# Carrying D·xn in PSUM ahead of Y, smaller first w1 loads, and a last group with tokens on partitions

## The chip, the cores and the metric

The kernel runs on one core of one Trainium2 chip. The metric is the device time of one execution in microseconds (us). A core has TensorE (PE), VectorE (DVE), ScalarE (ACT), GpSimd (POOL) and SyncE (SP, which only issues transfers here); they run their own instruction streams and meet through semaphores. PE multiplies into PSUM, an accumulator memory of 8 banks (ps0 to ps7) of 512 float32 columns; the other engines read and write PSUM and SBUF. DMA queues of SP and ACT move data between HBM and SBUF, and within SBUF with a transpose.

## The reference

x is 2048 tokens by 448 (bfloat16). A first normalization gives xn. One branch is a linear state-space scan over the tokens (448 complex states) with a skip term D, the other a normalized two-layer network, and the second gates the first:

```python
xn = _layernorm(x)                       # no weights; eps 1e-5
Lam_bar = exp(dt * Lam); B_bar = ((Lam_bar - 1) / Lam)[:, None] * B
h_t = Lam_bar * h_(t-1) + B_bar @ xn_t   # over 2048 tokens, complex
s = 2 * Re(C @ h_t) + xn * Dskip
g = silu(gelu(_layernorm(xn) @ w1 + b1) @ w2 + b2)   # 448 -> 1792 -> 448
out = x + s * g
```

## The kernel before

The tokens go in four groups of 512 (`g` = 0 to 3), each of two blocks of 256; a block is held as 128 partitions by two parities. Per group there are these stages, named by the letter that `STEPS` (L180 to L186) uses for them.

- L and N: normalization (`ln`), then a DMA transpose that puts the features on partitions: `xnT` for the scan branch, `xn2T` for the network.
- m: the first product, `mm1_phase` (matmuls L661, two phases into one pair of banks), with gelu by ACT out of PSUM into `gT` (L667).
- b: `bu_phase`, B·xn by PE (L690) with `BT`, the transposed matrix that `lb` and `bt` build (three DMA transposes: BT0, BT1, BT3, BT4 in two, and BT2, BT5, BT6 in the third); evacuated to `ue` and `u_sb`.
- S: `ssm` on DVE: table products, two scans (L749), products back into `hx`, and `hz` = hx + ue (L768).
- W: the second product, `mm2` (L783, and L786 for the last 64 features), features on partitions and 512 tokens as columns; ACT's silu with b2 as a bias column (L789) gives `g_sb`.
- Y: `yt`, for each of four blocks of features: 7 matmuls with `CZ` on hx (odd tokens, L805) and 7 with `CQ` on hz (even tokens, L806; L813 and L814 for the last 64 features). The skip term is added in one of two ways: DVE adds D·xn in a multiply-add out of PSUM into `tmp` (L826, thirteen of the sixteen), or PE adds a product with a diagonal matrix `Dg` of D (L808, L816: three of the last group). Then t3 = Y·g on DVE (L828).
- O and P: groups 0 to 2 leave by `out_dma`: two DMA transposes of t3 back to tokens, adds of x (L842, L845), stores. Group 3 leaves by `out_pe`: transposes on PE (L855), adds (L861), stores by SP and ACT in two pairs, the first of features 0 to 255, the last of 192 (rows of 384 bytes).

The gathering of work is written out in advance. Every operation is a task with the keys that it reads and writes (`Plan.add`); `ORDER` lists all task numbers once, each engine runs its tasks in that order, and `SECOND` names those that run on the second of two possible engines (`either`). So PE, in order, stands behind its first late input, and a transfer stands behind all that its queue has issued before. Just ahead of the fifth last task of SP (`settle`, L107), SP waits for all transfers that are under way.

The start: SP issues x, then w1 in five pieces (four column chunks of rows 0 to 383, `w1_0` to `w1_3`, and `w1r`, the rows 384 to 447 for all columns), then D and b2 as two rows (`drows`); ACT issues the three state vectors and b1. `skip_columns` (L554, L555) turns the two rows into columns `db` with small matmuls, which PE runs after the first 34 matmuls of the first product. `tables` makes the sine and decay tables `WT` under one key, "W"; the ten-step sine chain from L491 on runs on DVE.

## Time and profile before

| what | value |
| --- | --- |
| median of 3 runs | 147.08 us (147.01 to 148.35) |
| span of the profiled execution | 145.3 us |
| its own time beside the span | not recorded; the median lies 1.78 us above the span |
| busy: PE, DVE, ACT, POOL | 138.8, 130.1, 100.5, 26.0 us |
| the chain that ended last | PE 85%, DVE 4%, DMA 3%, SP's queue 3% |
| multiply-adds L826 on DVE | 16, 10.1 us, 645 ns each |
| moved by DMA | 15.98 MB, 110 GB/s over the span |

The profile is of one execution. A row of a group gives the line, the engine, the operation, output<-inputs, shapes and count, then the busy time and the mean of one in ns, then the idle time before them with what ended it. A row of a timeline begins with start and length in us; a bracket is the wait before it and what released it. A row of a window gives the busy time of each engine, the granted clock of PE (1.00 is full), the share of time that the DMA engines were busy, and GB/s. Matmuls overlap in the pipeline, so their own durations (380 ns for 512 columns) are longer than the step from one to the next (0.2145 us).

### The profile page before, as it was taken

Reading aid. Unit: us, or ns where it says so; the run is one execution under the profiler, and the core shown is the slowest. Engines: PE = TensorE matmul, PEld = TensorE weight load, DVE = VectorE, ACT = ScalarE, POOL = GpSimd, SP = SyncE. Lnnn points to the kernel's source line nnn. Section 1 sums busy time; section 2 is a strip of 40 time slices with the busy share of each in tenths; the row PEclk is TensorE's granted clock in tenths of the full one; section 3 lists DMA queues with packets and bytes.
Section 4 is the critical chain, followed back from the end, with each engine's and each line's share of the span. In section 5 each row is a group of like instructions: output and inputs, shape, how many; then the busy total and the mean of one; then the engine's idle time right before and its main releaser. Section 6 shows DMA issues by size and latency. Waiting matters only on the chain.

```text
span 145.3 us, 3626 instructions
## 1 busy us (share of the span) xinstructions
PE 138.8 (95%) x1457; PEld 91.9 (63%) x1461; DVE 130.1 (90%) x284; ACT 100.5 (69%) x184; POOL 26.0 (18%) x76
## 2 busy tenths in 40 slices
PE   7879999999999999999999999999999999999990
PEld 7757764464444477776768644877766668744870
DVE  2898999899999799899999999798699999999782
ACT  3588889998889466799999690594559993086200
POOL 4354315154500017000020000300000710000000
PEclk9999999999999999999999999999999999999999
DMA  4959990899999990000000074819800100201434
GB/s 104 299 173 242 351 366 19 162 226 95 210 210 215 122 241 11 5 2 5 0 0 5 18 144 89 163 23 187 192 7 0 68 0 0 82 4 23 95 116 126
DMA packets 38610, 15.98 MB, mean 110 GB/s; under 512 B 33145, under 2 KB 38146, under 8 KB 38594
## 3 DMA queue, kind: packets, MB, share of 16 engines
q1 hardware_dynamic: 38036, 15.52, 48.7%
q10 hardware_dynamic: 558, 0.24, 0.6%
q8 instruction: 11, 0.18, 0.5%
q14 instruction: 5, 0.04, 0.1%
HBM read 5.86 MB, written 1.84 MB: 53 GB/s over the span
## 4 chain that ended last, share of the span: by engine, by line
PE 85%; DVE 4%; DMA 3%; SPq 3%; issue 2%; DVEq 0%
PE psum L661 29%; PE psum L783 25%; PE psum L690 15%; PE psum L805 6%; PE psum L786 4%; PE psum L806 4%; DMA dk<-in_B_b_dram 3%; SPq L78 3%; PE psum L813 2%; DVE t L828 2%; DVE tmp L826 1%; DVE Bn L861 1%; DVE Bn L842 0%; PE psum L855 0%; PE psum L814 0%
## 5 line engine op out<-in xcount | busy, mean ns | idle before, releaser
L661 PE MATMUL psum<-xn2T,w_sb 64*128 64x512 bf16 (+1 forms) x476 | 46.7, 340 | 1.0 <-DVE w_sb L302 0.8
L667 ACT ACTIVATE gT<-psum,b1f 128x512 bf16<-128x512 f32 (+1 forms) x68 | 37.4, 615 | 5.2 <-PE psum L661 5.1
L783 PE MATMUL psum<-gT,w_sb 128*128 128x512 bf16 x164 | 36.2, 379 | 0.4 <-issue 0.3
L661 PEld LDWEIGHTS psum<-xn2T,w_sb 64*128 64x128 bf16 x476 | 25.3, 108 | 15.6 <-PE psum L661 1.4
L783 PEld LDWEIGHTS psum<-gT,w_sb 128*128 128x128 bf16 x168 | 16.2, 98 | 19.8 <-ACT gT L667 1.1
L690 PE MATMUL psum<-xnT,BT 64*128 64x256 bf16 x392 | 24.5, 270 | 0.2 <-DVE tmp L826 0.2
L690 PEld LDWEIGHTS psum<-xnT,BT 64*128 64x128 bf16 x392 | 18.9, 94 | 6.1 <-DVE tmp L826 0.4
L749 DVE TENSOR_TENSOR_SCAN s_w<-vs,dk 128x786 f32<-128x786 bf16 (+1 forms) x8 | 16.3, 2058 | 0.1
L443 ACT ACTIVATE xn_sb<-x_all,lnw 128x448 bf16<-128x448 bf16 (+2 forms) x18 | 11.2, 670 | 5.3 <-DMA xnT<-xn_sb 5.2
L301 ACT ACTIVATE vs<-s_w 64x258 bf16<-64x258 f32 (+2 forms) x12 | 8.0, 686 | 8.0 <-DVE s_w L749 7.9
L789 ACT ACTIVATE g_sb<-psum,db 128x512 bf16<-128x512 f32 (+1 forms) x16 | 9.3, 623 | 4.5 <-PE psum L783 4.4
L826 DVE SCALAR_TENSOR_TENSOR tmp<-xnT,db,psum 128x512 f32<-128x512 bf16 (+1 forms) x16 | 10.1, 645 | 0.9 <-PE psum L814 0.7
L805 PE MATMUL psum<-hx,CZ 128*128 128x256 bf16 x84 | 10.8, 276 | 0.0
L758 POOL TENSOR_TENSOR ang<-s_w,ang 128x16 f32<-128x16 f32 x3 | 1.8, 616 | 49.2 <-ACT s_w L756 49.2
L806 PE MATMUL psum<-Bn,CQ 128*128 128x256 bf16 x84 | 10.5, 273 | 0.0
L465 ACT ACT_TABLE_LOAD x8 | 10.3, 1283 | 0.3
L805 PEld LDWEIGHTS psum<-hx,CZ 128*128 128x128 bf16 x84 | 8.0, 98 | 2.5 <-issue 0.6
L301 ACT ACTIVATE ue<-psum 128x512 bf16<-128x512 f32 (+1 forms) x13 | 6.8, 549 | 3.6 <-PE psum L690 3.6
L806 PEld LDWEIGHTS psum<-Bn,CQ 128*128 128x128 bf16 x84 | 8.1, 98 | 1.4 <-issue 0.4
L301 ACT ACTIVATE u_sb<-psum 128x512 bf16<-128x512 f32 (+1 forms) x14 | 6.0, 490 | 3.5 <-PE psum L690 3.4
L828 DVE TENSOR_TENSOR t<-tmp,g_sb 128x512 bf16<-128x512 f32 (+1 forms) x13 | 7.9, 622 | 0.0
L442 DVE TENSOR_SCALAR xn_sb<-x_all,lnw 128x448 bf16<-128x448 bf16 (+2 forms) x22 | 7.2, 361 | 0.5 <-DMA xnT<-xn_sb 0.3
(155 smaller groups left out, 183.7 us busy)
## 6 DMA issues: line engine op xcount, KB each, us to landing
x_all<-in_A_x_dram SPq DMA_DIRECT2D x3, 448.0 KB, 4.6
w_sb<-in_B_w_dram SPq DMA_DIRECT2D x3, 448.0 KB, 6.4
out_dram<-Bn SPq DMA_DIRECT2D x6, 224.0 KB, 2.4
w_sb<-in_B_w_dram SPq DMA_DIRECT2D x3, 384.0 KB, 5.1
w_sb<-in_B_w_dram SPq DMA_DIRECT2D x2, 224.0 KB, 5.0
Bn<-in_A_B_im_dram SPq DMA_DIRECT2D x1, 336.0 KB, 7.5
Bn<-in_A_B_re_dram SPq DMA_DIRECT2D x1, 336.0 KB, 8.0
x_all<-in_A_x_dram SPq DMA_DIRECT2D x2, 112.0 KB, 2.0
```

Of the source, the lines that this page charges most:

```text
L301: kb.either(("act", [lambda e, o=o, i=i: e.activation(o, i, ACT.Copy) for o, i in pairs]), ("dve", [lambda e, o=o, i=i: e.tensor_copy(o, i ...
L443: ("act", [lambda e, o=o, i=i: e.activation(o, i, ACT.Identity, bias=nb, scale=rs) for o, i in parts]),
L465: kb.add("act", lambda e: e.preload_act_table_set(what), reads, writes, sem=name)
L661: return lambda e: e.matmul(dst(bk[k]), w1_sb[rows, d, fcol(2 * j + k)], rhs[rows, d], start=not second and n == 0, stop=second and n == 3)
L667: act(lambda e, k=k, fi=fi: e.activation(gT[:, gb, fi, cols], psum[:, bk[k], cols], ACT.Gelu_apprx_tanh, bias=b1f[:, fi:fi + 1]), ["b1f", ...
L690: fns.append(lambda e, rows=rows, bank=bank, m=m, o=o, n=n: e.matmul(psum[:, bank, c * NK:(c + 1) * NK].rearrange("p (b c) -> p b c", b=2) ...
L749: dve(lambda e, so=so, vi=vi, di=di: e.tensor_tensor_scan(so, vi, di, 0.0, ALU.add, ALU.mult), ["v", "vl", "vz", "dk", "dk01"] + ["v3"] * ...
L783: pe([lambda e, fi=fi: e.matmul(psum[:, bk, :], w2_sb[:, fi, 128 * j:128 * j + 128], gT[:, gb, fi, :], start=fi == 0, stop=fi == NF - 1) f ...
L805: pe([lambda e, k=k: e.matmul(par(psum[:, bk, :], 1), CZ[:, k, cols], halves(hx[:, hb, k, 1:NK + 1]), start=k == 0, stop=k == 6) for k in ...
L806: fns = [lambda e, k=k: e.matmul(par(psum[:, bk, :], 0), CQ[:, k, cols], halves(hz[:, hb, k, :]), start=not by_pe and k == 0, stop=not by_ ...
L826: dve([lambda e, o=o, p=p, x=x, d=d: e.scalar_tensor_tensor(out=v(o), in0=x, scalar=d, in1=v(p), op0=ALU.mult, op1=ALU.add) for o, p, x, d ...
L828: dve(lambda e: e.tensor_tensor(t3[:, 512 * j:512 * j + n], s, g_sb[:, hb, 512 * j:512 * j + n], ALU.mult), [ks, f"g{hb}_{j}"], [f"t3{j}"])
```

## The change

It has three parts, and a new order of everything.

1. In groups 0 to 2 the bank of Y is first written with D·xn, by ACT (ten of twelve: a copy with the D column as scale) or by DVE (two), and all matmuls then accumulate on it (`start=False`). The multiply-adds L826, the diagonal matrices `Dg` and their matmuls go; t3 is read out of PSUM.
2. `w1r` is loaded in two column pieces, 96 KB behind `w1_0` (192 KB, now first) and 128 KB behind `w1_2`. The rows of D and b2 are loaded on ACT's queue right behind b1. PE runs `skip_columns` five phases of the first product later.
3. In group 3 the second product has tokens on partitions: per quarter of 128 tokens, ACT copies a b2 row spread over all partitions into the bank, and 14 matmuls take `gT` as the stationary and w2 (448 columns) as the moving operand. Y too, in five pieces (three quarters whole, and the last in two halves of 224 columns): DVE writes D·xn into the bank, 7 matmuls add, then DVE multiplies by g and adds x, and each piece is stored at once (ACT stores one, SP four). No transposes are left in this group. The sum `hz` of group 3 is made in two halves. The spread rows come by two new loads on SP's queue in the middle of the kernel.

The order lists are new. What moves beside the above: the B products of group 0 (L690), which stood behind the second product of group 1, are split around it, the first twelve matmuls ahead of it, and those with BT2, BT5, BT6 first come after another twelve matmuls of that product; the B products of groups 1 and 2 stand earlier as well; on SP, the DMA transposes of `Ct3` and `CZ6` move from ahead of those of xnT and BT to behind them, and `Ct0` behind a load of x; the sine chain goes to POOL; one copy of w1 rows goes to ACT; the key "W" is split in five; `settle` is the fourth last task of SP, the store of the second piece.

```diff
-        settle = [t for t in order if t.eng == "sp"][-5]
+        settle = [t for t in order if t.eng == "sp"][-4]
...
-m2511 b1023 m2600 b1133 m2601 U2 L3 Y03d2 Y00d3 Y01d4 Y02d7 O0 N2 S1 W205 W216 W220 W231 Y13d2 Y10d3 Y11d4 Y12d7 O1 N3 G3 m3000 b2030 m3110 b2120
+m2511 b1023 m2600 b1133 m2601 U2 L3 Y032 Y003 Y014 Y027 O0 N2 S1 W205 W216 W220 W231 Y132 Y103 Y114 Y127 O1 N3 G3 m3000 b2030 m3110 b2120
-b3033 b3123 U3 Y23d2 Y20d3 Y21d0 Y22d1 O2 S3 W305 W316 W324 W337 Y33p2 P335 Y30d3 P306 Y31p0 P314 Y32p1 P327
+b3033 b3123 U3 Y232 Y203 Y210 Y221 O2 S3 W305 W316 W324 W337 Y3102 Y3303 Y3000 Y3211 Y3225
...
-        Dg = SB("Dg", [128, 4, 128])
...
+        rowsbc = tmp.bitcast(BF)
+        dbc, bbc = rowsbc[:, 0, 0:D], rowsbc[:, 1, 0:D]
+        w1f = w1_sb[:].rearrange("p k f -> p (k f)")
+        g3, y3, o3 = (w1f[:, 1792 * k:1792 * k + 1792].rearrange("p (q d) -> p q d", d=D) for k in range(3))
...
-            ld("sp", w1_sb[64:128, 3, :], dram_ap(B_w1, 384 * F, [[F, 64], [1, F]]), ["w1r"])
+            REST = ((0, 768), (768, 1024))
+
+            def ldrest(k):
+                a, w = REST[k]
+                ld("sp", w1_sb[64:128, 3, a:a + w], dram_ap(B_w1, 384 * F + a, [[F, 64], [1, w]]), [f"w1r{k}"])
+
             ldw1(0)
+            ldrest(0)
             ld("act", brows[0:3, :], dram_ap(B_b1, 256, [[512, 3], [1, 512]]), ["br0"], ["br"])
             ld("act", brows[3:4, 0:256], dram_ap(B_b1, 0, [[256, 1], [1, 256]]), ["br1"], ["br"])
-            for c in range(1, 4):
-                ldw1(c)
+            for i, vec in enumerate((A_Dskip, B_b2)):
+                ld("act", drows[i:i + 1, :], dram_ap(vec, 0, [[D, 1], [1, D]]), [f"dbr{i}"])
+            ldw1(1)
+            ldw1(2)
+            ldrest(1)
+            ldw1(3)
...
-            for i, vec in enumerate((A_Dskip, B_b2)):
-                ld("sp", drows[i:i + 1, :], dram_ap(vec, 0, [[D, 1], [1, D]]), [f"dbr{i}"])
...
-            def skips():
-                for j in range(4):
-                    small(lambda e, j=j: e.tensor_scalar(Dg[:, j, :], ident[:], dcol[:, j:j + 1], None, op0=ALU.mult), ["ident", "db"], [f"Dg{j}"])
...
-                        RA + ["rb", "Ws0", "sgn1", "sgn2", "sgn3"], ["W"] + (RA + ["rb"] if k == 4 else []))
+                        (["rb", "sgn3"] if k == 2 else RA + ["sgn1", "sgn2"]) + ["Ws0"], [f"W{k}"])
...
-                   xk2 + [f"w1_{c}", "w1r"] + ([f"w1c_{c}"] if second else []), [f"ps{bk[0]}", f"ps{bk[1]}"], split=True)
+                   xk2 + [f"w1_{c}", f"w1r{c // 2}"] + ([f"w1c_{c}"] if second else []), [f"ps{bk[0]}", f"ps{bk[1]}"], split=True)
...
-                dve(lambda e: e.tensor_tensor(hz[:, hb, :, :], hx[:, hb, :, 0:NK], ue[:, hb, :, :], ALU.add),
-                    [f"hx{hb}", f"hy{hb}"] + [f"ue{hb}{k}" for k in "abcd"] + ([f"BT{m}" for m in range(7)] if g < 2 else []), [f"hz{hb}"])
+                for k, cs in enumerate((slice(0, NK),) if g < NG - 1 else (slice(0, NK // 2), slice(NK // 2, NK))):
+                    dve(lambda e, cs=cs: e.tensor_tensor(hz[:, hb, :, cs], hx[:, hb, :, cs], ue[:, hb, :, cs], ALU.add),
+                        [f"hx{hb}", f"hy{hb}"] + [f"ue{hb}{k}" for k in "abcd"] + ([f"BT{m}" for m in range(7)] if g < 2 else []), [f"hz{hb}", f"hz{hb}{'ab'[k]}"])
...
-            def yt(g, j, by_pe, bk):
+            def yt(g, j, bk):
 
                 gx = hb = g % 2
-                ybank[0] += 1
                 n = 512 if j < 3 else NK
                 P = psum[:, bk, 0:n]
                 cols = slice(128 * j, 128 * j + 128) if j < 3 else slice(384, D)
                 xr = xnT[:, gx, :, j::4, :].rearrange("p b r c -> p (b r) c")
-                xt_k = [f"xnT{gx}"]
                 ko = [f"hx{hb}", f"hy{hb}"] + [f"CZ{k}" for k in range(7)]
                 ke = [f"hz{hb}"] + [f"CQ{k}" for k in range(7)]
+                seeds = [(P, xr, dcol[:, j:j + 1])]
+                if j == 3:
+                    seeds = [(P[h], xnT[h, gx, :, 4 * r + 3, :], dcol[h, 3:4]) for r, h in enumerate((slice(0, 64), slice(64, 128)))]
+                v = lambda t: t.rearrange("p (q c) -> p q c", c=128)
+                kb.either(("act", [lambda e, o=o, x=x, d=d: e.activation(v(o), x, ACT.Copy, scale=d) for o, x, d in seeds]),
+                          ("dve", [lambda e, o=o, x=x, d=d: e.tensor_scalar(v(o), x, d, None, op0=ALU.mult) for o, x, d in seeds]), ["db", f"xnT{gx}"], [f"ps{bk}"])
                 if j < 3:
-                    pe([lambda e, k=k: e.matmul(par(psum[:, bk, :], 1), CZ[:, k, cols], halves(hx[:, hb, k, 1:NK + 1]), start=k == 0, stop=k == 6) for k in range(7)], ko, [f"ps{bk}"])
-                    fns = [lambda e, k=k: e.matmul(par(psum[:, bk, :], 0), CQ[:, k, cols], halves(hz[:, hb, k, :]), start=not by_pe and k == 0, stop=not by_pe and k == 6, skip_group_check=by_pe) for k in range(7)]
-                    if by_pe:
-                        fns.append(lambda e: e.matmul(P.rearrange("p (q c) -> p q c", q=4), Dg[:, j, :], xr, start=False, stop=True, skip_group_check=True))
-                    pe(fns, ke + (xt_k + [f"Dg{j}"]) * by_pe, [f"ps{bk}"])
+                    pe([lambda e, k=k: e.matmul(par(psum[:, bk, :], 1), CZ[:, k, cols], halves(hx[:, hb, k, 1:NK + 1]), start=False, stop=k == 6, skip_group_check=True) for k in range(7)], ko, [f"ps{bk}"])
+                    pe([lambda e, k=k: e.matmul(par(psum[:, bk, :], 0), CQ[:, k, cols], halves(hz[:, hb, k, :]), start=False, stop=k == 6, skip_group_check=True) for k in range(7)], ke, [f"ps{bk}"])
                 else:
                     fns = []
                     for k in range(7):
-                        fns += [lambda e, k=k: e.matmul(psum[0:64, bk, 0:NK], CQ[:, k, cols], hz[:, hb, k, :], start=k == 0, stop=not by_pe and k == 6),
-                                lambda e, k=k: e.matmul(psum[64:128, bk, 0:NK], CZ[:, k, cols], hx[:, hb, k, 1:NK + 1], start=k == 0, stop=not by_pe and k == 6)]
-                    if by_pe:
-                        fns += [lambda e, r=r: e.matmul(halves(psum[64 * r:64 * r + 64, bk, 0:NK]), Dg[:, 3, 64 * r:64 * r + 64], xnT[:, gx, :, 4 * r + 3, :], start=False, stop=True) for r in range(2)]
-                    pe(fns, ko + ke + (xt_k + ["Dg3"]) * by_pe, [f"ps{bk}"], split=True)
-                s, ks = P, f"ps{bk}"
-                if not by_pe:
-                    fb = ybank[0] % 2
-                    s, ks = yD[:, fb, 0:n], f"tmp{fb}"
-                    parts = [(s, P, xr, dcol[:, j:j + 1])]
-                    if j == 3:
-                        parts = [(s[h], P[h], xnT[h, gx, :, 4 * r + 3, :], dcol[h, 3:4]) for r, h in enumerate((slice(0, 64), slice(64, 128)))]
-                    v = lambda t: t.rearrange("p (q c) -> p q c", c=128)
-                    dve([lambda e, o=o, p=p, x=x, d=d: e.scalar_tensor_tensor(out=v(o), in0=x, scalar=d, in1=v(p), op0=ALU.mult, op1=ALU.add) for o, p, x, d in parts],
-                        [f"ps{bk}", "db"] + xt_k, [ks])
-                dve(lambda e: e.tensor_tensor(t3[:, 512 * j:512 * j + n], s, g_sb[:, hb, 512 * j:512 * j + n], ALU.mult), [ks, f"g{hb}_{j}"], [f"t3{j}"])
+                        fns += [lambda e, k=k: e.matmul(psum[0:64, bk, 0:NK], CQ[:, k, cols], hz[:, hb, k, :], start=False, stop=k == 6, skip_group_check=True),
+                                lambda e, k=k: e.matmul(psum[64:128, bk, 0:NK], CZ[:, k, cols], hx[:, hb, k, 1:NK + 1], start=False, stop=k == 6, skip_group_check=True)]
+                    pe(fns, ko + ke, [f"ps{bk}"], split=True)
+                dve(lambda e: e.tensor_tensor(t3[:, 512 * j:512 * j + n], P, g_sb[:, hb, 512 * j:512 * j + n], ALU.mult), [f"ps{bk}", f"g{hb}_{j}"], [f"t3{j}"])
...
-            summed = set()
-
-            def out_pe(g, j, bank):
-
...
+                    pe([lambda e, k=k: e.matmul(P, hz[:, hb, k, ts], CQ[:, k, cs], start=False, stop=k == 6, skip_group_check=True) for k in range(7)],
+                       [f"hz{hb}{'ab'[b]}"] + [f"CQ{k}" for k in range(7)], [f"ps{bk}"])
+                dve(lambda e: e.tensor_tensor(y3[:, q, cs], P, g3[:, q, cs], ALU.mult), [f"ps{bk}", f"g3_{q}"], [f"y3_{q}{part}"])
+                dve(lambda e: e.tensor_tensor(o3[:, q, cs], y3[:, q, cs], x_all[:, 2 * g + b, r, cs], ALU.add), [f"y3_{q}{part}", f"x{2 * g + b}"], [f"o3_{q}{part}"])
+                kb.dma("act" if part == 1 else "sp", dram_ap(out, (2 * g + b) * 256 * D + r * D + cs.start, [[2 * D, 128], [1, n]]), o3[:, q, cs], reads=[f"o3_{q}{part}"], writes=[f"out{g}{q}{part}"])
...
-            skips()
...
+            spread_rows()
...
...
```

72 lines of the change are left out of this document (42 added, 30 removed), and 36 rows, old and new, of the table ORDER.

## The prediction

> **What bounds the kernel now.** I read the page's totals and its chain first.
>
> ```profile
> span 145.3 us, 3626 instructions
> ...
> PE 138.8 (95%) x1457; PEld 91.9 (63%) x1461; DVE 130.1 (90%) x284; ACT 100.5 (69%) x184; POOL 26.0 (18%) x76
> ...
> PE 85%; DVE 4%; DMA 3%; SPq 3%; issue 2%; DVEq 0%
> ```
>
> TensorE (PE) is busy for 138.8 of 145.3 us and is 85% of the chain; VectorE (DVE) has 90%. Busy shares over stages hide where PE waits, so the second view cuts the span at the events that the change touches (busy us by PE, weight load, DVE, ACT, POOL; then granted clock, DMA share, GB/s).
>
> ```profile
> 0.00:7.50 7.50, 5.89 (x66) 5.33 (x66) 4.35 (x15) 3.53 (x12) 2.89 (x20) 1.00 0.76 206
> ...
> 9.67:10.48 0.81, 0.00 (x1) 0.03 (x2) 0.78 (x4) 0.81 (x3) 0.65 (x3) 1.00 0.00 0
> 10.48:53.30 42.82, 42.31 (x391) 24.00 (x395) 39.67 (x126) 35.60 (x63) 12.14 (x35) 1.00 0.98 203
> 53.30:97.59 44.29, 44.08 (x488) 30.43 (x490) 41.80 (x70) 34.59 (x62) 6.42 (x12) 1.00 0.23 44
> 97.59:118.48 20.89, 20.89 (x283) 14.28 (x284) 18.93 (x29) 15.05 (x30) 3.01 (x4) 1.00 0.34 79
> 118.48:134.82 16.34, 16.29 (x127) 10.45 (x129) 16.12 (x25) 7.86 (x12) 0.00 (x0) 1.00 0.12 29
> 134.82:142.30 7.48, 7.17 (x75) 5.76 (x72) 6.13 (x12) 1.05 (x2) 0.00 (x0) 1.00 0.33 92
> 142.30:145.40 3.10, 0.00 (x0) 0.00 (x0) 0.27 (x1) 0.00 (x0) 0.00 (x0) 0.92 0.52 148
> ```
>
> From 10.48 to 134.82 PE is idle for 0.51+0.21+0.00+0.05 = 0.77 us. So taking work from DVE or ScalarE (ACT) there is worth at most 0.8 us. What PE loses lies in a 0.81 us hole at 9.67, in 0.3 us of the tail, and in 3.10 us at the end. Only three things can move the time: that hole, PE's own work, and what follows the last group's second product. The median of the runs, 147.08, is 1.78 us above this span; I add 1.78 to a span. Within 1% (what a measurement can tell) is 145.61 to 148.55.
>
> **The start.** Third view: the chain, PE's and DVE's timelines, and the loads' landings.
>
> ```profile
> 2.67 0.59 SPq L78
> 5.42 4.92 DMA dk<-in_B_b_dram
> w_sb<-in_B_w_dram SPq DMA_DIRECT2D x2, 224.0 KB, 5.0
> 2.24 0.24 ACTq L78 DMA_DIRECT2D dk<-in_B_b_dram  x1
> 7.54 2.13 PE L661 MATMUL psum<-xn2T,w_sb 64*128 64x256 bf16 x34 [0.82 <-DVE w_sb L302]
> 10.48 0.21 PE L554 MATMUL psum<-ident,dk 2*128 2x2 bf16 x3 [0.81 <-DMA dk<-in_B_b_dram]
> ```
>
> The product that turns the rows of D and b2 into columns (L554) waits for the b2 row: issued last of the first loads, 5.42, landed 4.92 later. Afterwards both rows are issued on ACT's queue right behind b1's second row (2.24+0.24), so before 3 us; with 4.92 they land near 8. The product also moves behind five more first-layer phases. The hole closes: 0.81 us. Who is late next? PE's first real matmul, 7.54, waited last for DVE by its row, and for the rest of w1, 224 KB issued at 2.67 that land in 5.0, so near 7.6 too. Afterwards its weights are a 192 KB and a 96 KB piece issued first, so they come earlier, but two small DVE steps are moved ahead of DVE's copy of the transposed x; the one more load costs SP an issue (0.59) that only the later weights feel. So no gain there, and the absolute value of the sine, now ahead of the gelu table on ACT, can cost the first gelu 0.2. The start is worth −0.5 to −0.8; I take −0.75.
>
> **Seeds in place of multiply-adds.** By shape, the removed and the nearest operations:
>
> ```profile
> L826 DVE SCALAR_TENSOR_TENSOR tmp<-xnT,db,psum 128x512 f32<-128x512 bf16 (+1 forms) x16 | 10.1, 645 | 0.9 <-PE psum L814 0.7
> L301 ACT ACTIVATE ue<-psum 128x512 bf16<-128x512 f32 x10 | 6.0, 598 | 3.6 <-PE psum L690 3.6
> L594 ACT ACTIVATE tmp<-Bn,cw 128x512 f32<-128x512 bf16 x1 | 0.7, 709 | 0.0
> L302 DVE CAST ue<-psum 128x512 bf16<-128x512 f32 x2 | 1.4, 685 | 0.0
> 12.47 0.17 DVE L491 TENSOR_SCALAR ang<-ang 128x16 f32<-128x16 f32 x1
> 14.36 0.18 DVE L497 TENSOR_TENSOR ang<-ang 128x16 f32<-128x16 f32 x1
> ```
>
> DVE loses 16 multiply-adds, 10.1 us, and the ten-step sine chain that goes to POOL, 12.47 to 14.54 = 2.07. It gains two seeds (0.685 each, the cast's price; split halves add a little), say 1.5. ACT gains ten seeds: no row shows a copy into PSUM with a scale, so the bounds are 0.598 (eviction) and 0.709 (scaled copy to f32), middle 0.65, 6.5 us in all, and four b2 copies, 2.4. None of it is on PE's path as long as each seed is done before PE's order reaches the bank; ACT has 9.7 idle us in 53.30:97.59, where most of the seeds of the first two groups fall. What DVE saves cannot be banked beyond the 0.77 us of PE holes; I take −0.2, range 0 to −0.5.
>
> **The first group's B products moved up.** This is the one edit that adds a wait.
>
> ```profile
> L77 SPq DMA_TRANSPOSE BT<-Bn x3: 1868/2627/4122, 38.7 to 43.3; - x3
> DMA to landing us min/median/max: 4.5/5.1/8.0
> L77 SPq DMA_TRANSPOSE Cr<-in_A_C_im_dram x2: 1156/1624/2092, 30.0 to 31.2; - x2
> L77 SPq DMA_TRANSPOSE CZ<-in_A_C_re_dram x1: 1258/1258/1258, 33.4 to 33.4; - x1
> DMA  0999999619999999999999999999994003999999
> 23.24 1.24 DVE L442 TENSOR_SCALAR xn_sb<-x_all,lnw 128x384 bf16<-128x384 bf16 x4
> 42.49 9.15 PE L783 MATMUL psum<-gT,w_sb 128*128 128x512 bf16 x41 [0.16 <-issue]
> 53.21 3.23 PE L690 MATMUL psum<-xnT,BT 64*128 64x256 bf16 x56
> ```
>
> Now PE uses the transposed B at 53.21, behind the second product of group 1. The three transposes are issued from 38.7 to 43.3 and land at 38.7+4.5 = 43.2, at about 45.7 (38.7+1.87, the first one's issue, +5.1) and at 43.3+8.0 = 51.3, so all are in time. Afterwards the first 12 of these matmuls stand ahead of that product, at 42.49−0.75 = 41.74, and the ones with the last transpose 12 of them (3.23/56 each, 0.69) and 12 of the product (9.15/42 each, 2.6) later, at 45.0. Ahead of the three on SP's queue two transposes are taken out, the C matrix's of 128 columns (1.16, the shorter of its two) and 1.26: 2.4. The queue's block of transposes starts when DVE has ended the normalized x at 24.48; the start (0.75) and the sine (2.07) bring that forward by up to 2.8, of which I count 1.5 to 2.8, since the loads ahead on the queue come no earlier than the start does. So all moves by 3.9 to 5.2: the second lands at 40.5 to 41.8 (needed 41.74) and the last at 46.1 to 47.4 (needed 45.0), a wait of 1.1 to 2.4. Against the longer one: the DMA digits of 36 to 54 (40 slices of 0.45) are full up to 49.5 and empty from 49.95 on, so the data were through at some 49.9 and the landing told 1.4 later; by that the wait is 0 to 1.0. Bounds 0 and 2.4; I take +0.8, nearer to the second, which PE, in order, does not win back. The two transposes moved behind feed the C matrices, first used by Y more than 20 us later, and the two new broadcast rows on SP are used in the last group alone: no cost. Queued behind the waiting matmul is all of PE; behind it ACT's evictions and the scan of group 0, which have slack until the first Y.
>
> **The last group and the tail.** The chain's tail and the last stores:
>
> ```profile
> 121.82 1.53 PE psum L786 x28
> 125.82 9.01 PE psum L783 x41
> 134.67 1.08 DVE L768 TENSOR_TENSOR Bn<-hx,ue 128x1792 bf16<-128x1792 bf16 x1
> 136.55 0.56 DVE L842 TENSOR_TENSOR Bn<-Cr,x_all 128x768 bf16<-128x768 bf16 x1 [0.80 <-DMA Cr<-t]
> 136.41 0.76 PE psum L806 x7
> 138.97 0.69 DVE t L828
> 142.28 0.29 DVE Bn L861
> out_dram<-Bn SPq DMA_DIRECT2D x1, 96.0 KB, 2.1
> out_dram<-Bn ACTq DMA_DIRECT2D x1, 96.0 KB, 2.4
> ```
>
> From the last B product (118.48) to the end are 26.8 us now: 16.36 to the end of the second product (125.82+9.01), and then Y, transposes back, adds and stores. The product is 42 matmuls of 512 columns, 9.01/42 = 0.2145 each, and 28 half ones, 1.53: 10.54 together. With tokens it is 4×14 of 448 columns, 0.188 each: 10.5. No gain: Y of group 2, 16.36−10.54 = 5.8, plus 10.5 ends it 16.3 after 118.48. Y is then 21 matmuls of 448 and 14 of 224: 21×0.188+14×0.094 = 5.25, ending at +21.6. Now 0.76 for 7 of 256, so about the same matmuls, but the D matmuls and 14 transposes go, and the serial DVE chain of 138.97 to 142.57 (3.6 us) shrinks to what hangs on the last half quarter: a multiply (0.69·224/512 = 0.30) and an add (about 0.25, by 0.29 for 256 columns). A store is then 2.1 (SP) to 2.4 (ACT) to landing, with 0.1 to issue and 0.3 to the end of the span. That makes 21.6+0.55+2.8 = 25.0, a gain of 1.8, if DVE is in time. DVE is busy for 16.12 of 16.34 in that stage: it loses five multiply-adds (5×0.645 = 3.2) and gains seeds of 0.6, 0.3 and 0.6 (the cast's price by columns), so hz starts about 1.7 before its present 134.67, at +14.5. Behind come group 2's add (0.55), half of hz (0.54), a seed (0.6), an add, a seed: +17.3, against PE's need at 16.3+1.3 = +17.6. That is level, with 0.3 to spare, and a wait of up to 0.8 if one of the DVE adds waits for its transpose. Lastly SP waits for all earlier transfers before the second of the last stores, so it cannot issue before the first has landed; with 2.1 and DVE's first part ready at about +19.2 that is +21.4, and the rest follow at 0.33 each, near the end anyway: 0.2. I take −1.5, bounds −2.0 and −0.3.
>
> The last two stores have rows of 448 bytes. The Trainium skill, "DMA: Bandwidth & Descriptors", Specifications, says that below 512 bytes a transfer does a read-modify-write and misses line rate. By that the last pieces (56 KB) might take twice their data time, at the last window's 148 GB/s 0.4 us more, for a time of 145.8. The trace does not bear it out: its last stores have rows of 384 bytes and land in 2.1 and 2.4.
>
> **The sum.** −0.75 −0.2 +0.8 −1.5 = −1.65: a span of 143.65, a time of 145.4, 1.1% less.
>
> **Rivals.**
> 1. Tail eaten (within 1%). DVE, not PE, sets the last group: its share is 16.12 of 16.34, seeds stand behind hz on it, and the wait of SP then comes later. For it speaks that nothing was idle there; against, the 3.2 us that go. Gain 0.3 instead of 1.5: 146.6.
> 2. ACT becomes late (within 1%). It has 35.60 of 42.82 and 34.59 of 44.29, and a seed queued behind gelus holds back PE and with it DVE. Ten seeds of which three come 0.4 late: +1.2, 146.6. Against: PE never waits for ACT in these windows now.
> 3. Slower: the last transpose of B is late. If it lands where it does now, 51.3, PE stands from 45.0: +6.3 less what the sum holds already, 145.4+5.5 = 150.9. It takes the sign above 148.55 from a wait of 4.0 on, a landing at 49.0. For it: 8.0 to landing now, with the DMA share at 0.98 up to 53.30; against: 2.4 us of queue taken out ahead, and nothing put in.
> The Trainium skill, "TensorE: Matmul & The Clock Gate", What's actually happening, adds that after about 3.4 us of idling PE drops to half clock for as long again; rival 3 would then be worse by some 1.7, 152.6. No wait here tests it: the clock is 1.00 over the 0.81 us hole.
>
> **Chances and range.** The forecast 0.62 (143.8 to 146.4, since its wait of 0 to 2.4 is open; 0.52 below 145.61, 0.10 above), rival 1 0.15, rival 2 0.12 (0.02 of it slower, if more seeds are late), rival 3 0.11 (0.10 slower, 0.01 within). Faster 0.52, same 0.36, slower 0.12. The range takes the best of each term, −0.8−0.5+0−2.0 = −3.3, 143.8, and up to rivals 1 and 2 with the longer wait, 145.4+1.2+1.0 = 147.6.
>
> **What will show it.** No wait of L554 for its rows; PE busy from 7.5 on without the hole. L690's first wait, if any, named as DMA of BT near 42 or 45: under 2.4 the sum holds, above 4 rival 3 has won. The seeds' row at 0.60 to 0.71 on ACT, and PE's idle before Y named ACT or DVE only below 0.3. In the tail the span from the last L690 to the end 25.3; a PE hole before the second Y piece, named DVE, is rival 1. The forecast is wrong if the middle windows lose more than 1 us to any wait that is not BT's.

## The result, and the profile after

| | before | after | ratio, 95% interval |
| --- | --- | --- | --- |
| first comparison | 147.93 us (147.01 to 148.47, 7 runs) | 146.22 us (145.42 to 147.66, 7 runs) | 0.9876 [0.9844, 0.9908] |
| second, another chip | 147.56 us (146.95 to 148.95, 29 runs) | 146.66 us (145.71 to 147.73, 12 runs) | 0.992 [0.9879, 0.9961] |

The change makes the kernel 0.8 to 1.2% faster. That it is faster is settled by both intervals; whether by more than 1% is not. The forecast was 145.4. The page of the kernel after begins so:

```profile
span 144.5 us, 3516 instructions
...
PE 137.4 (95%) x1404; PEld 89.1 (62%) x1408; DVE 124.9 (86%) x271; ACT 106.3 (74%) x198; POOL 24.0 (17%) x82
...
PE 80%; DMA 7%; ACT 7%; SPq 2%; issue 1%; DVE 1%; DVEq 0%
```

DVE has lost 5.2 us of work and ACT gained 5.8, and the chain shows it: DVE is down from 4% to 1%, while DMA and ACT hold 7% each. PE's timeline from its first real matmul on says where (start and length in us; the bracket is the wait before it):

```profile
7.27 0.50 PE L673 MATMUL psum<-xn2T,w_sb 64*128 64x256 bf16 x6
9.19 2.56 PE L673 MATMUL psum<-xn2T,w_sb 64*128 64x256 bf16 x42 [1.42 <-DMA w_sb<-in_B_w_dram]
11.69 0.22 PE L569 MATMUL psum<-ident,dk 2*128 2x2 bf16 x3
...
14.10 7.29 PE L673 MATMUL psum<-xn2T,w_sb 64*128 64x512 bf16 x106 [0.40 <-DMA xn2T<-xn_sb]
21.55 9.01 PE L796 MATMUL psum<-gT,w_sb 128*128 128x512 bf16 x41 [0.16 <-issue]
...
43.10 0.82 PE L702 MATMUL psum<-xnT,BT 64*128 64x256 bf16 x12
44.07 2.54 PE L796 MATMUL psum<-gT,w_sb 128*128 128x512 bf16 x11 [0.16 <-ACT gT L679]
46.54 2.58 PE L702 MATMUL psum<-xnT,BT 64*128 64x256 bf16 x44
```

The column product (L569) stands 14 matmuls later than before, which are two phases of the first product and not five, and waits for nothing: the old hole of 0.81 is gone. But PE runs six matmuls and then stands 1.42 us for the next piece of w1, and later 0.40 for the transposed x, which landed at 14.06 (12.71 before). The second product of group 0 starts at 21.55, not at 20.68. At 43.10 and 46.54, the places of the forecast BT wait, there is none. The windows at the corresponding events, and the tail; the first three rows are of the kernel before:

```profile
20.68 9.01 PE L783 MATMUL psum<-gT,w_sb 128*128 128x512 bf16 x41 [0.16 <-issue]
118.41 0.96 PE L805 MATMUL psum<-hx,CZ 128*128 128x256 bf16 x7
7.54:20.68 13.14, 12.04 (x187) 9.56 (x189) 12.41 (x55) 10.70 (x27) 5.44 (x17) 1.00 0.88 277
...
7.27:21.55 14.28, 12.18 (x187) 9.52 (x189) 11.69 (x51) 11.62 (x29) 10.76 (x43) 1.00 1.04 295
...
97.60:119.55 21.95, 21.82 (x297) 14.51 (x294) 18.06 (x27) 16.14 (x35) 1.64 (x3) 1.00 0.26 60
119.55:135.70 16.15, 16.15 (x114) 10.30 (x113) 15.57 (x25) 10.36 (x18) 0.00 (x0) 1.00 0.27 48
135.70:141.20 5.50, 5.48 (x36) 3.31 (x34) 5.07 (x12) 0.54 (x1) 0.00 (x0) 1.00 0.14 52
141.20:144.50 3.30, 0.00 (x0) 0.00 (x0) 0.78 (x4) 0.00 (x0) 0.00 (x0) 1.00 0.51 172
```

From 119.55 to 141.20 PE is not idle for more than 0.02 us; the last 3.30 are the last multiply, add and store. So the span is cut in three, in two profiles of each kernel:

| stretch | before | before again | after | after again |
| --- | --- | --- | --- | --- |
| to the second product of group 0 | 20.68 | 20.56 | 21.55 | 21.55 |
| from there to the first Y matmul of group 2 | 97.7 | 97.7 | 98.0 | 99.15 |
| from there to the end | 26.9 | 26.9 | 24.95 | 24.9 |
| span | 145.3 | 145.2 | 144.5 | 145.6 |

The whole gain is in the last stretch, 1.95 us; the start gives 0.9 to 1.0 back, and the middle 0.3 or 1.4. The two pairs of profiles differ by −0.8 and +0.4; over all runs of the second chip the mean span falls by 0.8, from 145.8 to 145.0. A second part of the gain lies outside the span. Over all runs a time lies 2.05 us above its span before (29 runs) and 1.72 after (12 runs). The prediction's 1.78 had set the median of three runs against a profile that did not belong to the median; it lies near the 1.72 of the kernel after by chance.

### The profile page after: what moved, and what is told of

Same layout as the page of the kernel before. It is cut to its first block, busy times and chain, and to the rows that moved or that the text cites. A ratio compares the mean times of both kernels' runs of the same rounds, so it can differ in the third digit from the quotient of the medians.

```text
span 144.5 us, 3516 instructions
## 1 busy us (share of the span) xinstructions
PE 137.4 (95%) x1404; PEld 89.1 (62%) x1408; DVE 124.9 (86%) x271; ACT 106.3 (74%) x198; POOL 24.0 (17%) x82
## 3 DMA queue, kind: packets, MB, share of 16 engines
HBM read 6.09 MB, written 1.84 MB: 55 GB/s over the span
## 4 chain that ended last, share of the span: by engine, by line
PE 80%; DMA 7%; ACT 7%; SPq 2%; issue 1%; DVE 1%; DVEq 0%
PE psum L673 23%; PE psum L796 19%; PE psum L702 13%; PE psum L857 7%; PE psum L820 5%; PE psum L821 5%; ACT gT L679 4%; DMA w_sb<-in_B_w_dram 4%; DMA xn2T<-xn_sb 4%; PE psum L799 3%; PE psum L870 2%; PE psum L825 2%; SPq L78 2%; PE psum L873 1%; ACT ue L304 1%
## 5 line engine op out<-in xcount | busy, mean ns | idle before, releaser
L796 PE MATMUL psum<-gT,w_sb 128*128 128x512 bf16 x122 | 27.0, 379 | 0.6 <-issue 0.5
L796 PEld LDWEIGHTS psum<-gT,w_sb 128*128 128x128 bf16 x126 | 12.0, 97 | 14.8 <-issue 0.8
L457 DVE TENSOR_SCALAR xn_sb<-x_all,lnw 128x448 bf16<-128x448 bf16 (+2 forms) x31 | 9.9, 366 | 1.3 <-DMA xn2T<-xn_sb 1.2
L857 PE MATMUL psum<-w_sb,gT 128*128 128x448 bf16 x56 | 10.9, 352 | 0.0
L828 DVE TENSOR_TENSOR t<-psum,g_sb 128x512 bf16<-128x512 f32 (+1 forms) x12 | 7.3, 615 | 1.8 <-PE psum L821 1.7
L857 PEld LDWEIGHTS psum<-w_sb,gT 128*128 128x128 bf16 x56 | 5.5, 98 | 4.8
L820 PE MATMUL psum<-hx,CZ 128*128 128x256 bf16 x63 | 8.1, 275 | 0.0
L821 PE MATMUL psum<-Bn,CQ 128*128 128x256 bf16 x63 | 7.9, 272 | 0.0
L817 ACT ACTIVATE psum<-xnT,db 128x512 f32<-128x512 bf16 (+1 forms) x12 | 7.4, 628 | 0.1
L375 DVE BATCH_NORM_STATS2 lnst<-x_all 128x6 f32<-128x448 bf16 x12 | 7.1, 608 | 0.0
```

The costliest lines, as they stand in the source:

```text
L457: kb.either(("dve", [lambda e, o=o, i=i: e.tensor_scalar(o, i, rs, nb, op0=ALU.mult, op1=ALU.add) for o, i in parts]), ("act", [lambda e, ...
L796: pe([lambda e, fi=fi: e.matmul(psum[:, bk, :], w2_sb[:, fi, 128 * j:128 * j + 128], gT[:, gb, fi, :], start=fi == 0, stop=fi == NF - 1) f ...
L817: kb.either(("act", [lambda e, o=o, x=x, d=d: e.activation(v(o), x, ACT.Copy, scale=d) for o, x, d in seeds]), ("dve", [lambda e, o=o, x=x ...
L820: pe([lambda e, k=k: e.matmul(par(psum[:, bk, :], 1), CZ[:, k, cols], halves(hx[:, hb, k, 1:NK + 1]), start=False, stop=k == 6, skip_group ...
L821: pe([lambda e, k=k: e.matmul(par(psum[:, bk, :], 0), CQ[:, k, cols], halves(hz[:, hb, k, :]), start=False, stop=k == 6, skip_group_check= ...
L857: pe([lambda e, fi=fi: e.matmul(P, gT[:, gb, fi, 128 * q:128 * q + 128], w2_sb[:, fi, :], start=False, stop=fi == NF - 1, skip_group_check ...
```

## The experiments

Twelve kernels, in three groups, each group on one chip with its own runs of the kernel before. Ratios are to these.

### The tail alone, and the change without it

The third part alone on the kernel before (`Dg` dropped, the spread rows in a buffer of their own):

```diff
-b3033 b3123 U3 Y23d2 Y20d3 Y21d0 Y22d1 O2 S3 W305 W316 W324 W337 Y33p2 P335 Y30d3 P306 Y31p0 P314 Y32p1 P327
+b3033 b3123 U3 Y23d2 Y20d3 Y21d0 Y22d1 O2 S3 W305 W316 W324 W337 Y3102 Y3303 Y3000 Y3211 Y3225
```

> The kernel before with the third part alone: group 3 with tokens on partitions, b2 and D*xn written into PSUM first, no transposes, stores by quarter; the diagonal matrices, no longer used, are gone; all else and the order ahead of it as before. Theory (the tail's form is worth 1.95 us only if DVE is in time, which needs the seeds of group 2): PE waits up to 1.3 us for DVE before the second piece, and the last B product to the end takes 25.6 to 26.4 us instead of 26.84: span 144.4 to 144.9. Rival (the form alone gives all of it): from the last B product to the end 24.9, span 143.4, 1.3% faster than before.

Measured: 150.22 us, ratio 1.0139 [1.0079, 1.0199]: slower, where both theories had it faster. From the first Y matmul of group 2 (118.28) to the end are 30.4 us instead of 26.9. PE's timeline, then a row of DVE's:

```profile
139.53 2.13 PE L875 MATMUL psum<-CQ,Bn 128*128 128x448 bf16 x7 [3.00 <-DVE psum L870]
141.46 2.58 PE L872 MATMUL psum<-CZ,hx 128*128 128x448 bf16 x7
...
136.84 0.56 DVE L844 TENSOR_TENSOR Bn<-Cr,x_all 128x768 bf16<-128x768 bf16 x1 [1.58 <-DMA Cr<-t]
```

Without seeds the multiply-adds of group 2 still stand in DVE's queue. They make t3 late, its transpose late, and DVE then waits 1.58 us for that transpose with the seed for PE's second Y piece queued behind. PE stands 3.00 us, and its granted clock behind that is 0.62 (139.5 to 144). This is rival 1, come true. That the missing seeds are the reason, and not the old order, is shown by the run below that takes away those of group 2 alone.

The reverse: the kernel after with its first two parts, and group 3 in the old form (its D·xn also seeded, by ACT).

```diff
-b3033 b3123 U3 Y232 Y203 Y210 Y221 O2 S3 W305 W316 W324 W337 Y3102 Y3303 Y3000 Y3211 Y3225
+b3033 b3123 U3 Y232 Y203 Y210 Y221 O2 S3 W305 W316 W324 W337 Y332 P335 Y303 P306 Y310 P314 Y321 P327
```

> The kernel after with its first two parts alone: group 3's second product, Y and transposes by TensorE in the old form, with D*xn of group 3 seeded too (by ScalarE). Theory A (the tail's new form is what the gain consists of, the seeds only make it possible): 147.7 to 148.3, from TensorE's first Y matmul of group 2 to the end 26.3 to 27.0 us, ratio to before 0.998 to 1.005. Theory B (the seeds gain by themselves, as multiply-adds leave VectorE): 146.4 to 147.2, ratio 0.990 to 0.995.

Measured: 147.83 us, ratio 0.9993 [0.9956, 1.003]; the kernel after beside it 146.66. From its first Y matmul of group 2 (119.71) to the end (146.2) are 26.5 us. Theory A holds: seeds and loads by themselves gain nothing, the new tail is the gain, and by the run before this, and the one on group 2 below, it needs the seeds.

### The seeds

All seeds of groups 0 to 2 undone in the kernel after; D·xn is multiplied and added behind Y, in place in PSUM:

```diff
-                kb.either(("act", [lambda e, o=o, x=x, d=d: e.activation(v(o), x, ACT.Copy, scale=d) for o, x, d in seeds]),
-                          ("dve", [lambda e, o=o, x=x, d=d: e.tensor_scalar(v(o), x, d, None, op0=ALU.mult) for o, x, d in seeds]), ["db", f"xnT{gx}"], [f"ps{bk}"])
...
+                dve([lambda e, o=o, p=p, x=x, d=d: e.scalar_tensor_tensor(out=v(o), in0=x, scalar=d, in1=v(p), op0=ALU.mult, op1=ALU.add) for o, p, x, d in parts],
+                    [f"ps{bk}", "db", f"xnT{gx}"], [f"ps{bk}"])
```

> The changed kernel without its first part: in groups 0 to 2 no seeds; the first matmuls of a bank start it anew and DVE adds D*xn by a multiply-add in place in PSUM, ahead of the product with g. Theory (seeds are worth little in the middle, where PE does not wait, and decide the tail, where DVE was level with PE with 0.3 us to spare): DVE has 5 multiply-adds, 3.2 us less 1.5 of seeds, more in the last stage, so PE waits some 1.3 us before the second Y piece; the transposes of xn also wait for the multiply-adds now, which can cost the B products of groups 2 and 3 up to 1.5 us: span 145.8 to 147.3. Rival (the seeds move nothing that matters): span 144.2 to 144.9.

Measured: five executions of 158.32 to 162.53 us and one of 500.5 (before 147.97), far outside of either. So two more kernels took the seeds away by groups. Groups 0 and 1 only:

> The kernel after with the seeds of groups 0 and 1 undone in the same way; group 2 keeps its seeds. Theory A (most of the 12 us that were lost without any seed come from xnT: its buffer is read by the multiply-adds, so the transposes of groups 2 and 3 are issued 10 to 15 us later, and TensorE and VectorE wait for them): 152 to 158, with waits of TensorE for xnT and of VectorE's normalisation for xnT. Theory B (the loss sits in the tail, behind group 2's seeds): 146.5 to 148.5.

Measured: 158.64 us, four executions of 155.86 to 158.96 (before 147.33). Theory A; the median is a little above its range, the fastest execution inside. PE's waits, then a row of DVE's timeline, in an execution with a span of 157.2:

```profile
PE psum L828 <- DVE hx L785: 5.6, 1, 5.6
PE psum L708 <- DMA xnT<-xn_sb: 2.1, 1, 2.1
...
93.27 0.70 DVE L463 TENSOR_SCALAR xn_sb<-x_all,lnw 128x448 bf16<-128x448 bf16 x2 [4.31 <-DMA xnT<-xn_sb]
```

The multiply-add reads `xnT`, and there are two buffers of it for four groups. A seed reads it before Y; a multiply-add after Y. In the kernel after the DMA transposes of xnT for groups 2 and 3 are issued at 78.92 and 94.47, here at 88.99 and 110.95. DVE stands 4.31 us on the first of them, and PE 5.6 and 2.1. The kernel before had the same long hold (88.11 and 97.58), but an order in which the B products came late enough. The new order puts them early and lives from the release. Part of the rest of the loss is the clock: behind the two long waits the granted clock is 0.81, 0.85 and 0.83 over 90 to 100, 100 to 110 and 110 to 120 us. No run gave xnT a third buffer, so how much the release alone is worth is read from these waits, not measured apart.

Group 2 only (`own = g == 2`, otherwise the same edit):

> The kernel after with the seeds of group 2 alone undone: its four D*xn are multiplied and added by VectorE behind Y, in place in PSUM; groups 0 and 1 keep their seeds. Theory A (the tail needs VectorE free: it had 0.3 to 0.5 us to spare at the second Y piece of group 3, and gets three multiply-adds of about 0.65 more and loses one seed of 0.99 for another multiply-add): TensorE waits 1.2 to 3 us ahead of Y pieces of group 3, 147.4 to 149.5. Theory B (the seeds matter only because they release xnT in groups 0 and 1): 146.0 to 146.8.

Measured: 148.57 us, ratio 1.0085 [1.0049, 1.0122]. Theory A:

```profile
137.85 1.50 PE L881 MATMUL psum<-CZ,hx 128*128 128x448 bf16 x7 [0.77 <-DVE hx L785]
140.41 1.50 PE L884 MATMUL psum<-CQ,Bn 128*128 128x448 bf16 x7 [1.05 <-DVE psum L879]
```

PE waits 1.82 us ahead of Y's first two pieces; from the first Y matmul of group 2 (120.49) to the end (147.9) are 27.4 us, 2.5 more than with the seeds. What the tail saves hangs on 1.8 us of DVE's time (126.7 us busy here, 124.9 with the seeds).

### The start

The old split and order of w1 in the kernel after (the rows of D and b2 stay on ACT; PE's first phases in the old order):

```diff
-            REST = ((0, 768), (768, 1024))
+            REST = ((0, 1792),)
...
-            ldrest(1)
```

> The changed kernel with the loads of w1 as they were: rows 384 to 447 in one piece, order w1_1, w1r, w1_0, w1_2, w1_3 on SP, and PE's first three products (with ACT's gelus and one copy of w1 on DVE) in the old order; the rows of D and b2 stay on ACT's queue. Theory (the start lost because w1_1 was issued third, behind a 192 KB and a 96 KB piece, and landed at 9.15 instead of 6.43): PE's wait of 1.42 us for w1 at 7.8 goes, the old hole at 9.7 does not come back, and the second product of group 0 starts at 19.9 to 20.3 instead of 21.55: span 142.9 to 143.3, time 1.2 to 1.6 us below the changed kernel's. Rival 1 (the two small row loads on ACT's queue slow the w1 loads down): w1 still lands near 9 and the wait stays, span 144.2 to 144.8. Rival 2 (the next gate, the transposed x that lands at 14.06, takes over): span 143.6 to 144.2.

Measured: 147.26 us, ratio 0.996 [0.9923, 0.9998]. It did not get faster, against a forecast of 1.2 to 1.6 us; one of twelve executions took 183.03. Here the old split waits too, and more is lost: the window behind it is at a granted clock of 0.57 (columns as above).

```profile
8.60 4.23 PE L678 MATMUL psum<-xn2T,w_sb 64*128 64x256 bf16 x42 [1.66 <-DMA w_sb<-in_B_w_dram]
...
8.00:12.00 4.00, 3.40 (x34) 2.77 (x34) 1.96 (x7) 3.02 (x8) 1.42 (x6) 0.57 0.36 115
```

The rows of D and b2 on ACT's queue, in the kernel before:

```diff
-                ld("sp", drows[i:i + 1, :], dram_ap(vec, 0, [[D, 1], [1, D]]), [f"dbr{i}"])
+                ld("act", drows[i:i + 1, :], dram_ap(vec, 0, [[D, 1], [1, D]]), [f"dbr{i}"])
```

> The kernel before with one edit: the rows of D and b2 are loaded on ACT's queue behind b1. Theory (only the rows' late issue made the hole): no wait at 9.7, the second product of group 0 starts at 19.9 to 20.1 instead of 20.68, span 144.5 to 144.8 instead of 145.3, 0.3 to 0.5% faster. Rival 1 (small loads on a second queue slow w1): the first product starts later than 7.54 by 0.3 or more and nothing is gained. Rival 2 (the next gate, transposed x, landing 12.7, holds PE): 0.3 us gained.

Measured: 146.92 us, ratio 0.9979 [0.9943, 1.0015]. The hole is gone, and the second product of group 0 starts at 20.30: of the 0.81 us, 0.38 arrive. The time shows no difference that the interval can tell.

The whole second part in the kernel before: the new pieces and their order, the rows on ACT, PE's first phases in the order of the pieces. The edit is the loads' part of the diff shown with the change.

> The kernel before with the second part alone: w1 in the new pieces and order (w1_0, the 96 KB rest, w1_1, w1_2, rest, w1_3), the rows of D and b2 on ACT's queue, and TensorE's first phases in the order of these pieces. Theory A (the new split protects the start: the kernel after lost 1.04 us of its median when it got the old split back, and the kernel before gained 1.0 us on its own median when the rows moved): about 146.0 to 146.6, ratio to before 0.987 to 0.992. Theory B (the start's gain is kept only together with the seeds and the tail, what starts earlier stalls later behind DVE): 147.2 to 148.0, ratio 0.995 to 1.000, with TensorE's waits in the middle longer by what the start gained.

Measured: 148.19 us, ratio 1.0057 [1.0018, 1.0095]: a little slower, which neither theory had. In its profile the second product of group 0 starts at 20.50 and the first Y of group 2 at 118.46, as before; no gain to be seen.

The rows back on SP's queue, in the kernel after (the one-line edit of the rows, reversed):

> The kernel after with the two rows of D and b2 loaded by SP again, behind w1_3, as before. Theory A (the hole of 0.81 us at the column transposes comes back, as forecast): TensorE waits 0.5 to 0.9 us there, 146.5 to 147.0. Theory B (the time that the hole takes is covered by the later wait for the transposed x, which is 0.40 us already): 146.0 to 146.5, with the wait for xn2T gone.

Measured: 146.93 us, ratio 0.9905 [0.9863, 0.9948], against 0.992 for the kernel after on the same chip: no difference. PE's waits in this profile, and in that of the kernel after again:

```profile
PE psum L575 <- DMA dk<-in_B_b_dram: 2.3, 1, 2.3
...
PE psum L679 <- DMA w_sb<-in_B_w_dram: 0.5, 1, 0.5
```

```profile
PE psum L673 <- DMA w_sb<-in_B_w_dram: 1.3, 1, 1.3
PE psum L673 <- ACT gT L679: 1.1, 1, 1.1
...
PE psum L673 <- DVE w_sb L305: 0.3, 1, 0.3
```

The hole is 2.3 long, and yet both reach the first Y of group 2 at the same time, 120.63 and 120.70. What the rows cost, waits for w1 and for ACT's gelu cost otherwise. Theory A has the hole right, though not its size, and its time of 146.5 to 147.0; but beside the kernel after, 146.66 on this chip, nothing is lost. Theory B's reason, a wait for the transposed x, is in neither profile.

### The kernel after again, and before again

> The kernel after, unchanged, timed beside the kernel before on a second chip, with a second profile. Theory A (the tail's form and the seeds are worth about 1.7 us wherever the first loads land): ratio to before 0.985 to 0.991, about 146.0 to 146.4, from TensorE's first Y matmul of group 2 to the end 24.9 us again (26.84 before). Theory B (the gain depends on how unluckily the first loads of before land): ratio 0.991 to 0.998. For both: if w1_1 lands before 8.5 in this profile, TensorE's second product of group 0 starts before 21.0, against 21.55 in the first profile.

Measured: ratio 0.992 [0.9879, 0.9961], between the two theories' ranges; the last stretch is 24.9 us again. And w1_1 landed at 7.85, yet the second product of group 0 started at 21.55 as in the first profile. So the last expectation, which both theories shared, was wrong: it is not w1_1 alone that sets this. Timelines of DVE, PE, POOL and ACT:

```profile
12.97 0.29 DVE L305 COPY w_sb<-w_sb 64x512 bf16<-64x512 bf16 x1 [2.27 <-DMA w_sb<-in_B_w_dram]
...
12.99 8.40 PE L673 MATMUL psum<-xn2T,w_sb 64*128 64x256 bf16 x126 [1.30 <-DMA w_sb<-in_B_w_dram]
...
37.06 7.35 PE L673 MATMUL psum<-xn2T,w_sb 64*128 64x512 bf16 x64 [1.07 <-ACT gT L679]
...
24.36 0.50 POOL L618 COPY Bn<-Bn 128x384 bf16<-128x384 bf16 x1 [2.98 <-DMA Bn<-in_A_B_re_dram]
...
24.89 0.72 ACT L606 ACTIVATE tmp<-Bn,cw 128x512 f32<-128x512 bf16 x1 [1.37 <-POOL Bn L618]
```

w1_3, the last piece, landed at 12.95 (11.52 in the first profile). PE stood 1.30 us for it and DVE, which copies 64 of its rows, 2.27. The loads issued behind w1 were late too: the real part of B landed at 24.24 (21.92), so POOL's copy of it came at 24.36 (22.04), and ACT stood 1.37 us for that copy, for which it had not waited in the first profile. ACT began its gelus of group 1 at 35.74 instead of 34.59, and PE stood 1.07 us for them. That is the 1.1 us between the two spans of the same kernel. Its twelve spans fall into six of 144.0 to 144.5 and six of 145.4 to 146.0.

> The kernel before, unchanged, for a second profile. Theory A (the spread of the unchanged kernel's spans, 144.9 to 145.4 and 145.7 to 146.6, comes from when w1 lands): with a span over 145.7 TensorE waits 1.2 us or more for w1, or its granted clock is lower behind that wait, and the second product of group 0 starts at 21.2 or later instead of 20.68; with a span below 145.4 it starts at 20.3 to 20.8. Theory B: the start is as in the first profile and the spread comes from a later wait.

Measured: a span of 145.2, and the second product of group 0 at 20.56. This agrees with theory A, but the spans above 145.7 of the kernel before have no profile, so their cause stays open.

### The B transposes

The kernel after with the transposes of Ct3 and CZ6 ahead of those of xnT and BT on SP's queue again. No code changes, only the order (the tasks are written here by their names):

```diff
-SP: Ct0 Ct4 xnT0 BT1 BT0 BT2 Ct3 CZ6
+SP: Ct0 Ct3 Ct4 CZ6 xnT0 BT1 BT0 BT2
```

> The kernel after with the transposes of Ct3 and CZ6 put back ahead of xnT0 and the three BT transposes on SP's queue, as before; nothing else. Theory A (moving these two behind BT is what made the last BT land at 45.3 and so took away the wait that I had forecast at 0.8 us): the last BT lands 1.6 to 2.4 us later, at 46.9 to 47.7, against TensorE's need at 46.6: a wait of 0.3 to 1.1 us, 146.5 to 147.3. Theory B (BT's landing goes by the transfers ahead of it, not by the order on the queue): the last BT lands at about 45.3, no wait, 146.0 to 146.4.

Measured: 146.83 us, ratio 0.9938 [0.9903, 0.9974], not told apart from the kernel after. The rows of BT's transposes (durations of the issue; first and last start) and of PE:

```profile
L77 SPq DMA_TRANSPOSE BT<-Bn x3: 1892/2851/4265, 36.4 to 41.3; - x3
...
43.98 0.83 PE L708 MATMUL psum<-xnT,BT 64*128 64x256 bf16 x12 [0.60 <-DMA BT<-Bn]
```

The first transpose is issued at 36.4 instead of 32.9, of which 0.9 is a later start of the whole block of transposes (27.9 for 27.1). The rest, 2.7, is the two that stand ahead. The second transpose lands at 43.85 instead of 41.33 and PE waits 0.60 us for it, at the first B products; for the third, which theory A had named, it does not wait. So without the two moves there is a wait of this kind; the forecast of 0.8 had counted them in.

## Why the prediction was right, and where it was not

The time (146.22 for 145.4, inside 143.8 to 147.6) and the sign were right. The size was not: the sum was −1.65 on the span; measured on the profile is 144.5 − 145.3 = −0.8. That the two medians of the first comparison differ by 1.71, much as forecast, is luck: 0.3 of it lies outside the span, in no term, and on the second chip they differ by 0.90. The range was wide, too: beside 147.08 it reached from a gain of 3.3 to a loss of 0.5. Term by term:

| term | forecast | measured |
| --- | --- | --- |
| start | −0.75 | +0.87 |
| seeds in the middle, and the BT wait | −0.2 + 0.8 = +0.6 | +0.3 (+1.4 in the second profile) |
| tail | −1.5 | −1.95 |

**The start** failed, in sign. The hole closed as forecast. The step that failed is "the one more load costs SP an issue (0.59) that only the later weights feel. So no gain there". PE feels the later weights as well: the small first piece feeds six matmuls, and w1_1, issued third at 3.26 instead of first at 2.19, was the next that PE needed. In the second profile w1_1 was in time and w1_3 took its place, to the same 21.55. The windows show the loss: PE is idle for 13.14 − 12.04 = 1.10 us of the old stretch (7.54 to 20.68) and for 14.28 − 12.18 = 2.10 of the new. And no row had been quoted for who else waits when w1 is late: DVE does, and ACT, through the load of B behind it. Four profiles with the old split ahead of the old order have all of w1 at 9.8 to 10.4; eight with the new split in the new order have it at 11.5 to 13.0; the one with the new split in the old order and the one with the old split in the new order have it at 10.9 each, so both have a part in it. The runs on the parts agree that the start brings nothing: 0.9979 for the rows alone, 1.0057 for rows and split, and no difference when the rows go back. How much of the time the new split by itself costs is not settled, since undoing it in the kernel after did not help either (0.996 against 0.9876 to 0.992).

**The seeds** were priced inside their bounds and valued wrongly. By shape, from the groups of the kernel after:

```profile
L817 ACT ACTIVATE psum<-xnT,db 128x512 f32<-128x512 bf16 x8 | 5.7, 707 | 0.0
L817 ACT ACTIVATE psum<-xnT,db 64x256 f32<-64x256 bf16 x4 | 1.9, 469 | 0.0
```

A seed takes 0.707, at the upper of the two bounds, 0.598 and 0.709, not at the middle 0.65. Ten of them are 7.5 us, not 6.5, and no matmul waited for one, so rival 2 did not come; the 1.07 us for ACT in the second profile were for gelus that a load had made late. "What DVE saves cannot be banked" holds for the kernel before with its old order: the change without its tail gains nothing. But the step saw only DVE's time. Undone, the seeds of groups 0 and 1 cost 9 to 12 us, by the waits behind the late release of xnT and the clock after them, which was no term of the sum, and those of group 2 cost 2.5 us in the tail.

**The BT wait** was 0 instead of 0.8, inside its bounds, in part by luck. The first of these transposes was issued 38.7 − 32.9 = 5.8 us earlier, where 3.9 to 5.2 were counted, but not for the reasons counted. The block of transposes started 0.9 earlier (its first issue at 23.57 for 24.51), where the start and the sine were to bring 1.5 to 2.8. The two transposes moved behind were worth 2.7 us, by the run with them ahead, for 2.4. Most of the rest is a term that was not there, the issue of xnT's transpose in the same block, before and after:

```profile
34.67 3.98 SPq L77 DMA_TRANSPOSE xnT<-xn_sb  x1
...
30.89 1.92 SPq L77 DMA_TRANSPOSE xnT<-xn_sb  x1
```

And the need came later with the late start, at 43.10 and 46.54 for 41.74 and 45.0; the landings were 41.33 and 45.32. Rival 3 was far off: the third landing is 1.2 us ahead of its use.

**The tail** went as worked out, to a tenth: the second product ended 16.3 after the first Y matmul, Y 21.6, the end 24.95. DVE's second seed and PE's use of it, forecast at +17.3 and +17.6:

```profile
136.09 0.63 DVE L868 TENSOR_TENSOR psum<-xn_sb,tmp 128x448 f32<-128x448 bf16 x1
...
135.70 1.49 PE L870 MATMUL psum<-CZ,hx 128*128 128x448 bf16 x7
137.03 1.49 PE L873 MATMUL psum<-CQ,Bn 128*128 128x448 bf16 x7
```

The seed ends at 136.72, PE starts at 137.03: +17.2 and +17.5, 0.3 to spare. The 0.3 that was taken off for a wait of DVE and for SP's settling did not come. Rival 1 stayed away by 0.3 us only; both runs that give DVE work back in group 2 turn into it. By the Trainium skill, "DMA: Bandwidth & Descriptors", Specifications, the last stores with rows below 512 bytes might have taken 0.4 more, by the prediction's estimate. The trace does not settle it. These two landed in 1.9 and 2.1 us, no later than the 2.1 and 2.4 of the sum; but the three stores ahead of them, twice as large and with rows of 896 bytes, took 1.7:

```profile
out_dram<-w_sb SPq DMA_DIRECT2D x3, 112.0 KB, 1.7
...
out_dram<-w_sb ACTq DMA_DIRECT2D x1, 56.0 KB, 1.9
out_dram<-w_sb SPq DMA_DIRECT2D x1, 56.0 KB, 2.1
```

The last two overlapped with each other and with another store, so the 0.2 to 0.4 has more than one possible reason.

## What to carry to other kernels

Ask of a removed operation not only whose time it frees but which buffer it held and until when: here most of what PE waited for when it was undone came from the late release. Parts of a change that each gain nothing, or lose, may gain together, so price the new form's thinnest margin (0.3 us of DVE here) with and without the other parts. When a load is cut so that its first piece comes sooner, price its last piece, every engine that stands in order behind that, and the loads queued behind it.
